# First group of a fused attention and expert kernel: keys pooled on TensorE, scores in a double bank, first two weight halves unpacked behind the first exponentials

## The chip, the cores and the metric

The kernel runs on one core of a Trainium2 chip. The metric is the device time of one execution in microseconds; lower is better. Engines are named as in the profile: PE (TensorE's matrix products) with PEld (its weight loads), DVE (VectorE), ACT (ScalarE), POOL (GpSimd), SP (the engine that issues the DMAs).

## What is computed

Three stages follow each other: attention over keys and values that are averaged in groups of eight, a dense two-layer network with a softplus, and a mixture of eight experts of which each token takes one.

```python
k_p = k.reshape(B, H, Sp, pool, D).mean(axis=3)      # pool = 8, Sp = 72, D = 64
v_p = v.reshape(B, H, Sp, pool, D).mean(axis=3)
scores = scale * np.matmul(q, k_p.transpose(0, 1, 3, 2))
attn = np.exp(scores - np.max(scores, axis=-1, keepdims=True))
attn = attn / (np.sum(attn, axis=-1, keepdims=True) + 1e-09)
x = np.matmul(attn, v_p)                             # 4608 tokens x 512
h = x @ w_in                                         # 512 x 2048
g = np.maximum(h, 0.0) + np.log1p(np.exp(-np.abs(h)))
x = g @ w_out                                        # 2048 x 512
...
y[mask] = gate_w[mask, None] * (np.maximum(xc[mask] @ w1[e], 0.0) @ w2[e])
```

## The kernel before, in words

The 4608 tokens are worked on in nine groups of 512. A group's attention consists of four **units** (`unit0` for the first group, `unit` for the others), each for two heads. A unit loads a key block of 128 x 576 and the queries, averages the keys (`keys`, L527: a DVE reduction over eight neighbours, L530), spreads the result over a block-diagonal tile (two ACT copies, L537 and L538) and forms the scores with PE (L585 in the first group, L635 later). DVE takes maxima (L593) and subtracts them (L594); `shares` (L541) has ACT's exponential (L542), DVE's sum, addition and reciprocal (L543 to L545) and POOL's multiplication (L546). In the first group PE averages the values by eight products with the identity (`pv`, L603) and transposes the shares by products with the identity (`tr`, L612); ACT copies both out of PSUM (L605, L613). `output` (L565) forms the unit's result `o` (L569), which ACT and DVE split into a rounded part `xh` and a remainder `xl` (L571, L572).

A group's dense network runs over 16 chunks of 128 hidden columns. For each, `p1` forms the hidden product in twelve matmuls (L715), ACT and DVE compute the softplus (L718 to L721) and split it (L723, L725), and `p2`, two chunks behind, adds to four output banks (L736 to L738). The bank of a hidden product comes from the pool `ps_h`, of two; it comes free when DVE's L721 has read it. In the first group that pool also holds `pv` and `o`.

The dense weights come as 64-bit words and are turned into pairs of float32 tiles while the first group is at work: `load_weights` is a generator. Its function `half` handles 512 columns of a chunk: a DMA of 512 KB (L485), two ACT unpackings (L469, L471), two DVE joins (L474, L476), an ACT copy (L491) and a DVE subtraction (L493). Chunks 4 to 15 go in pairs of 1,024 columns through the same operations (DMA L506, copy L519, subtraction L520), and two left-over halves at the end. `weights(n)` advances that generator by n steps, `STEPS` in all, and `ready(c)` tells how many steps chunk c needs.

The instructions are written in the order of these generators; a scheduler puts them into each engine's queue when the program is built, and each engine works off its queue in order. Waits are by semaphores. The order of each queue can be printed, and the section on the change does so. Lines below are those of the kernel before.

## Time and profile before

| what | value |
|---|---|
| runs shown | 1370.27, 1370.47, 1371.11 us |
| median | 1370.47 us |
| the profiled execution's own time | 1378.22 us |
| its span, first to last instruction | 1376.5 us |
| mean granted clock of TensorE | 0.994 |
| PE / PEld / DVE / ACT / POOL busy | 97% / 81% / 62% / 43% / 22% of the span |

The profile is of one execution, whose time lies 7.75 us above the median of the runs shown. Busy shares are means over the whole span, and the first hundred microseconds, in which the first group's attention and the conversion of the weights run, differ from the rest. So the trace is asked by stretch below.

### The profile page before, as it was taken

The page shows a single profiled execution, that of the slowest core. Times are in us where ns is not written, and L with a number is a line of the kernel's source. Part 1 is how long each engine was busy: PE and PEld are TensorE (multiplying, and loading weights), DVE is VectorE, ACT ScalarE, POOL GpSimd, SP SyncE. Part 2 cuts the span into 40 slices and gives each one's busy share as a digit, 9 for nine tenths or more (in the row PEclk, how much of TensorE's full clock was granted, in tenths as well). Part 3 has the DMA queues.
Part 4 walks back from the last instruction along what each step waited for, and adds up shares of the span by engine and source line. Part 5 has one row for each costly group of instructions (what it writes and reads, how often), then busy time and mean ns, then how long its engine had stood idle before and what let it go on. Part 6 is the DMA issues. An engine that isn't in the chain of part 4 may idle for free. (4 is left out here: it accounts for less than half of the span.)

```text
span 1376.5 us, 21364 instructions
## 1 busy us (share of the span) xinstructions
PE 1338.4 (97%) x7030; PEld 1114.9 (81%) x7030; DVE 847.6 (62%) x1951; ACT 594.6 (43%) x1076; POOL 309.6 (22%) x374
## 2 busy tenths in 40 slices
PE   6899999999999999999999999999999999999986
PEld 5667877777878778788778778888989898889886
DVE  7997794783974974965956847545645332325254
ACT  6985544544545545455455445541111121114142
POOL 2000012111121121030030120343424243323233
PEclk9999999999999999999999999999999999999998
DMA  8633343241241340431421301513323122225272
GB/s 283 260 115 90 86 136 75 59 130 48 76 125 35 80 129 26 112 106 31 118 70 33 106 13 47 192 39 92 96 70 100 57 76 67 81 61 169 64 269 80
DMA packets 149599, 134.16 MB, mean 97 GB/s; under 512 B 100789, under 2 KB 116789, under 8 KB 146912
## 3 DMA queue, kind: packets, MB, share of 16 engines
q1 hardware_dynamic: 131744, 95.51, 24.0%
q0 software_dynamic: 17728, 37.13, 8.5%
q8 instruction: 59, 0.97, 0.3%
q14 instruction: 68, 0.56, 0.1%
HBM read 166.67 MB, written 29.67 MB: 143 GB/s over the span
## 5 line engine op out<-in xcount | busy, mean ns | idle before, releaser
L715 PE MATMUL h<-xh,wt 128*128 128x512 f32 x1152 | 381.9, 393 | 3.4 <-DVE a L721 3.1
L715 PEld LDWEIGHTS h<-xh,wt 128*128 128x128 f32 x1152 | 217.6, 189 | 51.2 <-DVE a L721 4.9
L894 PE MATMUL h<-xt,w1h 128*128 128x256 f32 x1280 | 229.1, 282 | 4.2 <-ACT w1h L404 1.7
L736 PE MATMUL y<-wt,gh 128*128 128x512 f32 x576 | 233.2, 405 | 0.0
L119 DVE CUSTOM_DVE_ANT_0 junk<-rows,w9b 128x512 bf16<-128x512 f32 x324 | 223.0, 688 | 8.3 <-ACT rows L113 3.2
L715 PE MATMUL h<-xl,wt 128*128 128x512 f32 x576 | 225.7, 392 | 0.0
L737 PE MATMUL y<-wt,gh 128*128 128x512 f32 x576 | 225.4, 391 | 0.0
L738 PE MATMUL y<-wt,gl 128*128 128x512 f32 x576 | 224.7, 390 | 0.0
L894 PEld LDWEIGHTS h<-xt,w1h 128*128 128x128 f32 x1280 | 197.7, 189 | 9.2 <-issue 4.8
L894 PE MATMUL h<-xt,w1l 128*128 128x256 f32 x640 | 180.4, 282 | 3.8 <-issue 2.4
L898 ACT ACTIVATE hs<-h 128x512 fp32r<-128x512 f32 x80 | 47.6, 598 | 307.5 <-PE h L894 170.1
L718 ACT ACTIVATE a<-h 128x512 f32<-128x512 f32 x144 | 85.9, 597 | 184.1 <-PE h L715 172.4
L721 DVE SCALAR_TENSOR_TENSOR a<-h,a 128x512 f32<-128x512 f32 x144 | 98.5, 684 | 101.0 <-ACT a L720 100.4
L723 ACT ACTIVATE gh<-a 128x512 fp32r<-128x512 f32 x144 | 90.8, 630 | 158.5 <-DVE a L721 152.9
L736 PEld LDWEIGHTS y<-wt,gh 128*128 128x128 f32 x576 | 108.1, 188 | 36.5 <-ACT a L718 8.3
L715 PEld LDWEIGHTS h<-xl,wt 128*128 128x128 f32 x576 | 109.0, 189 | 22.9 <-issue 0.7
L738 PEld LDWEIGHTS y<-wt,gl 128*128 128x128 f32 x576 | 108.1, 188 | 23.7 <-DVE gl L725 0.4
L725 DVE TENSOR_TENSOR gl<-a,gh 128x512 fp32r<-128x512 f32 x144 | 99.2, 689 | 42.0 <-ACT gh L723 39.4
L894 PEld LDWEIGHTS h<-xt,w1l 128*128 128x128 f32 x640 | 122.7, 192 | 2.8 <-issue 1.0
L737 PEld LDWEIGHTS y<-wt,gh 128*128 128x128 f32 x576 | 108.3, 188 | 20.1 <-issue 0.4
L920 PE MATMUL y<-w2h,hs 128*128 128x512 f32 x304 | 118.4, 390 | 0.3 <-issue 0.3
L919 PE MATMUL y<-w2l,hs 128*128 128x512 f32 x304 | 118.4, 389 | 0.2 <-issue 0.2
(197 smaller groups left out, 1728.0 us busy)
## 6 DMA issues: line engine op xcount, KB each, us to landing
w9b<-w SPq DMA_DIRECT2D x81, 256.0 KB
raw<-wbits SPq DMA_DIRECT2D x12, 1024.0 KB
x2d<-rows SPq DMA_DIRECT2D x36, 260.0 KB
et<-q SPq DMA_DIRECT2D x256, 32.0 KB
kv<-kT SPq DMA_DIRECT2D x28, 288.0 KB
kv<-vT SPq DMA_DIRECT2D x28, 288.0 KB
xm<-misc SPq DMA_DIRECT2D x160, 32.0 KB
misc<-misc SPq DMA_DIRECT2D x144, 32.0 KB
```

Of the source, the lines that this page charges most:

```text
L119: nc.vector.tensor_tensor_reduce(out=ws["junk"], in0=rows[t][:, :D], in1=w9b[e], scale=1.0, scalar=0.0, op0=ALU.mult, op1=ALU.add, accum_o ...
L715: nc.tensor.matmul(h, lhsT=l, rhs=r[:, kk, :], start=n == 0, stop=n == 11)
L718: nc.scalar.activation(out=a, in_=h, func=AF.Abs)
L721: nc.vector.scalar_tensor_tensor(out=a, in0=h, scalar=0.0, in1=a, op0=ALU.max, op1=ALU.add)
L723: nc.scalar.activation(out=gh, in_=a, func=AF.Copy)
L725: nc.vector.tensor_tensor(out=gl, in0=a, in1=gh.bitcast(F32), op=ALU.subtract)
L736: nc.tensor.matmul(y, lhsT=th, rhs=wh, start=c == 0, stop=False)
L737: nc.tensor.matmul(y, lhsT=th, rhs=wl, start=False, stop=False)
L738: nc.tensor.matmul(y, lhsT=tl, rhs=wh, start=False, stop=c == 15)
L894: nc.tensor.matmul(h[:, f2, :], lhsT=l, rhs=r[:, kk, :], start=n == 0, stop=n == 11)
L919: nc.tensor.matmul(y, lhsT=hh[:, f, js], rhs=ws["w2l"][:, f, :], start=False, stop=False)
L920: nc.tensor.matmul(y, lhsT=hl[:, f, js], rhs=ws["w2h"][:, f, :], start=False, stop=f == 7)
```

## The change

In the first group, the keys are averaged by eight products with the identity on PE (`pk`, L606 of the new kernel) in place of the DVE reduction; the block-diagonal copies read that bank directly (`band`), and ACT also copies the averaged keys to SBUF for the later group that needs them (L609). All four score products of a unit go into one tile over two banks (pool `ps_s`), so that one DVE maximum (L622) and one subtraction (L623) serve the unit in place of two of each. The key products of a unit are put behind the scores of the unit before it, the value products behind the scores written last, and the unpacking of the first two weight halves behind the exponentials of the first two units (`issue_after`). The early weight halves are fetched two ahead (`fetch`), and the start advances the weights' generator in other places. The four output banks (`ps_y`) are now taken after the first group's attention has been written.

```diff
--- before.py
+++ after.py
@@ -427,7 +427,8 @@
         ep = ph.enter_context(tc.tile_pool(name="ep", bufs=1))
         ps_a = ph.enter_context(tc.tile_pool(name="ps_a", bufs=2, space=PSUM))
         ps_h = ph.enter_context(tc.tile_pool(name="ps_h", bufs=2, space=PSUM))
-        ps_y = ph.enter_context(tc.tile_pool(name="ps_y", bufs=1, space=PSUM))
+        ps_s_cm = tc.tile_pool(name="ps_s", bufs=2, space=PSUM)
+        ps_s = ps_s_cm.__enter__()
 
         kbd = []
         for i in range(2):
@@ -455,7 +456,7 @@
             return pool.tile([P, n], F32, tag=tag, name=tag)
 
         EARLY = 4
-        STEPS = 6 * EARLY + 6 * (8 - EARLY // 2)
+        STEPS = 2 + 6 * EARLY + 6 * (8 - EARLY // 2)
         scratch_cm = tc.tile_pool(name="scratch", bufs=2, side="right")
         scratch = scratch_cm.__enter__()
         wt = []
@@ -476,16 +477,22 @@
                 nc.vector.scalar_tensor_tensor(out=v, in0=hi, scalar=-0x80000000, in1=v,
                                                op0=ALU.bitwise_and, op1=ALU.bitwise_or)
 
-            def half(c, j, first):
+            def fetch(c, j):
+                raw = room("raw", 1024, True)
+                nc.sync.dma_start(out=raw.bitcast(I32), in_=bits[c * P:(c + 1) * P, j * 1024:(j + 1) * 1024])
+                return raw.bitcast(I32).rearrange("p (a b) -> p a b", b=2)
+
+            def half(c, j, raw):
                 wh, wl = (wt[c // 2][:, c % 2, i, j * 512:(j + 1) * 512] for i in range(2))
-                if first:
-                    raw = room("raw", 1024, True).bitcast(I32).rearrange("p (a b) -> p a b", b=2)
-                else:
+                if raw is None:
                     raw = scratch.tile([P, 512, 2], I32, tag="raw", name="raw")
-                nc.sync.dma_start(out=raw.rearrange("p a b -> p (a b)"),
-                                  in_=bits[c * P:(c + 1) * P, j * 1024:(j + 1) * 1024])
+                    nc.sync.dma_start(out=raw.rearrange("p a b -> p (a b)"),
+                                      in_=bits[c * P:(c + 1) * P, j * 1024:(j + 1) * 1024])
                 lo, hi = raw[:, :, 0], raw[:, :, 1]
-                unpack(lo, hi)
+                with ExitStack() as st:
+                    if c < 2 and j == 0:
+                        st.enter_context(tc.issue_after(firsts[c]))
+                    unpack(lo, hi)
                 yield
                 join(lo, lo, hi)
                 nc.scalar.activation(out=wh, in_=lo.bitcast(F32), func=AF.Copy)
@@ -496,9 +503,15 @@
 
             for i in range(EARLY // 2):
                 wt.append(wtile(i, f"wt{i}", 2, 2, 1024, dtype=F32R))
-            for c in range(EARLY):
-                for j in range(2 if c >= LAG else 1):
-                    yield from half(c, j, True)
+            early = [(c, j) for c in range(EARLY) for j in range(2 if c >= LAG else 1)]
+            raws = []
+            for i in range(2):
+                raws.append(fetch(*early[i]))
+                yield
+            for i, (c, j) in enumerate(early):
+                if i + 2 < len(early):
+                    raws.append(fetch(*early[i + 2]))
+                yield from half(c, j, raws[i])
             for i in range(EARLY // 2, 8):
                 raw = wtile(i, f"raw{i}", 2, 1024, 2, dtype=I32)
                 for j in range(2):
@@ -520,7 +533,7 @@
                     nc.vector.tensor_tensor(out=wl, in0=vs[j], in1=wh.bitcast(F32), op=ALU.subtract)
                     yield
             for c in range(LAG):
-                yield from half(c, 1, False)
+                yield from half(c, 1, None)
 
         pooled = {}
         count = [0]
@@ -531,15 +544,20 @@
                 v = kv()
                 nc.sync.dma_start(out=v, in_=vT[u])
                 pooled[u] = (kp, v, None)
-            kp = pooled[u][0]
+            return band(pooled[u][0])
+
+        def band(kp):
             kb = kbd[count[0] % 2]
             count[0] += 1
             nc.scalar.activation(out=kb[0:64, 0:SP], in_=kp[0:64, :], func=AF.Copy)
             nc.scalar.activation(out=kb[64:128, SP:2 * SP], in_=kp[64:128, :], func=AF.Copy)
             return kb
 
+        firsts, scores = [], []
+
         def shares(e, sm, rc):
-            nc.scalar.activation(out=e, in_=e, func=AF.Exp, scale=1.0 / 64)
+            ins = nc.scalar.activation(out=e, in_=e, func=AF.Exp, scale=1.0 / 64)
+            firsts.append(ins.ins)
             nc.vector.tensor_reduce(sm, e, AX.X, ALU.add)
             nc.vector.tensor_scalar_add(sm, sm, 1e-9)
             nc.vector.reciprocal(rc, sm)
@@ -579,28 +597,39 @@
             nc.sync.dma_start(out=q, in_=qT[u, :, r0:r0 + rn])
             yield
             yield
-            banks = [ps_y.tile([P, 512], F32, tag=f"y{hp % 2 * 2 + i}", name="s") for i in range(2)]
-            kb = keys(u, k, lambda: room("kv", 576, True))
+            k8 = k.rearrange("p (s w) -> p w s", w=8)
+            pk = ps_h.tile([P, 512], F32, tag="h", name="pk")[:, :SP]
+            with ExitStack() as after:
+                if scores:
+                    after.enter_context(tc.issue_after(scores[-1]))
+                for w in range(8):
+                    nc.tensor.matmul(pk, lhsT=ident, rhs=k8[:, w], start=w == 0, stop=w == 7)
+            kb = band(pk)
+            kp = pp.tile([P, SP], F32, tag="kp", name="kp")
+            nc.scalar.activation(out=kp, in_=pk, func=AF.Copy)
+            v = room("kv", 576, True)
+            nc.sync.dma_start(out=v, in_=vT[u])
+            s2 = ps_s.tile([P, 1024], F32, tag="s", name="s2")
             for t in range(T):
-                nc.tensor.matmul(banks[t // 3][:, t % 3 * 144:(t % 3 + 1) * 144],
-                                 lhsT=q[:, t * P:(t + 1) * P], rhs=kb, start=True, stop=True)
+                a = t // 2 * 512 + t % 2 * 144
+                ins = nc.tensor.matmul(s2[:, a:a + 144], lhsT=q[:, t * P:(t + 1) * P], rhs=kb, start=True, stop=True)
+            scores.append(ins.ins)
             e = k.rearrange("p (a k) -> p a k", k=SP)
             st = room("st", 24, True)
             mx, sm, rc = (st[:, i * 8:(i + 1) * 8] for i in range(3))
-            for b, (i, j) in enumerate(((0, 3), (3, 4))):
-                s3 = banks[b][:, :(j - i) * 144].rearrange("p (a k) -> p a k", k=SP)
-                m = mx[:, 2 * i:2 * j]
-                nc.vector.tensor_reduce(m, s3, AX.X, ALU.max)
-                nc.vector.tensor_tensor(out=e[:, 2 * i:2 * j], in0=s3, op=ALU.subtract,
-                                        in1=m.unsqueeze(2).to_broadcast([P, 2 * (j - i), SP]))
+            s4 = s2.rearrange("p (b x) -> p b x", b=2)[:, :, :288].rearrange("p b (a k) -> p b a k", k=SP)
+            m = mx.rearrange("p (b a) -> p b a", b=2)
+            nc.vector.tensor_reduce(m, s4, AX.X, ALU.max)
+            nc.vector.tensor_tensor(out=k.rearrange("p (b a k) -> p b a k", b=2, k=SP), in0=s4, op=ALU.subtract,
+                                    in1=m.unsqueeze(3).to_broadcast([P, 2, 4, SP]))
             shares(e, sm, rc)
             yield
             yield
-            kp, v, _ = pooled[u]
             v8 = v.rearrange("p (s w) -> p w s", w=8)
             pv = ps_h.tile([P, 512], F32, tag="h", name="pv")
-            for w in range(8):
-                nc.tensor.matmul(pv[:SP, :P], lhsT=v8[:, w], rhs=ident, start=w == 0, stop=w == 7)
+            with tc.issue_after(scores[-1]):
+                for w in range(8):
+                    nc.tensor.matmul(pv[:SP, :P], lhsT=v8[:, w], rhs=ident, start=w == 0, stop=w == 7)
             vp = pp.tile([SP, P], F32, tag="vp", name="vp")
             nc.scalar.activation(out=vp, in_=pv[:SP, :P], func=AF.Copy)
             pooled[u] = (kp, v, vp)
@@ -742,8 +771,8 @@
 
         def ready(c):
             if c < EARLY:
-                return 3 * (2 * c - min(c, LAG)) + 3
-            return 3 * (2 * EARLY - LAG) + 6 * ((c - EARLY) // 2) + 6
+                return 3 * (2 * c - min(c, LAG)) + 5
+            return 2 + 3 * (2 * EARLY - LAG) + 6 * ((c - EARLY) // 2) + 6
 
         def weights(n):
             for _ in range(n):
@@ -783,11 +812,14 @@
         feed.start(units_of(0), 1)
         for i, it in enumerate(feed.units):
             next(it)
-            if i:
+            if i % 2:
                 weights(1)
+        feed.tick()
         while feed.units or jobs:
             feed.tick()
-            weights(1)
+            weights(1 if feed.units else 2)
+        ps_s_cm.__exit__(None, None, None)
+        ps_y = ph.enter_context(tc.tile_pool(name="ps_y", bufs=1, space=PSUM))
 
         pend = []
         for g in range(NG):
```

**PE, the first group's attention up to the fourth unit's scores.** `s` are scores, `pk` and `pv` the poolings of keys and values, `tr` transposes, `o` results; a pooling and a score product each appear as twice as many instructions in the trace. Before:

```order
L585 MATMUL s<-kbd_165,boot 128x144 x4
L585 MATMUL s<-kbd_167,boot 128x144 x4
L612 MATMUL tr<-ident,boot_kv 72x128 x6
L603 MATMUL pv<-ident,boot_kv 72x128 x8
L585 MATMUL s<-kbd_165,boot 128x144 x4
L612 MATMUL tr<-ident,boot_kv 72x128 x2
L603 MATMUL pv<-ident,boot_kv 72x128 x8
L585 MATMUL s<-kbd_167,boot 128x144 x4
```

And now:

```order
L606 MATMUL pk<-boot_kv,ident 128x72 x8
L615 MATMUL s_203<-kbd_165,boot 128x144 x4
L606 MATMUL pk<-boot_kv,ident 128x72 x8
L615 MATMUL s_232<-kbd_167,boot 128x144 x4
L632 MATMUL pv<-ident,boot_kv 72x128 x8
L606 MATMUL pk<-boot_kv,ident 128x72 x8
L641 MATMUL tr<-ident,boot_kv 72x128 x8
L615 MATMUL s_272<-kbd_165,boot 128x144 x4
L632 MATMUL pv<-ident,boot_kv 72x128 x8
L606 MATMUL pk<-boot_kv,ident 128x72 x8
L641 MATMUL tr<-ident,boot_kv 72x128 x8
L615 MATMUL s_325<-kbd_167,boot 128x144 x4
```

Four key poolings stand ahead of the fourth scores that were not there, and the second unit's transposes have moved ahead of those scores; behind them the rest of the order is two value poolings, two sets of transposes and the results.

**DVE, between the third hidden chunk's L721 and the next (L750 in the new kernel).** L474 and L476 (now L475 and L477) are joins of 1,024 columns, L520 (now L533) the subtraction that ends a conversion, L653 (now L682) the transposes of a unit of the second group. Before:

```order
L721 SCALAR_TENSOR_TENSOR a<-h,a 128x512
L474 SCALAR_TENSOR_TENSOR v<-raw_516 128x1024
L653 STREAM_TRANSPOSE q<-q 128x768
L725 TENSOR_TENSOR gl<-a,gh 128x512
L476 SCALAR_TENSOR_TENSOR v<-raw_516,v 128x1024
L553 TENSOR_REDUCE vr<-kv 128x72
L520 TENSOR_TENSOR wt_567<-v,wt_567 128x1024 x2
L721 SCALAR_TENSOR_TENSOR a<-h,a 128x512
```

And now:

```order
L750 SCALAR_TENSOR_TENSOR a<-h,a 128x512
L563 RECIPROCAL st<-st 128x8
L477 SCALAR_TENSOR_TENSOR v<-raw_518,v 128x1024
L754 TENSOR_TENSOR gl<-a,gh 128x512
L682 STREAM_TRANSPOSE q<-q 128x768
L533 TENSOR_TENSOR wt_579<-v,wt_579 128x1024 x2
L475 SCALAR_TENSOR_TENSOR v<-raw_584 128x1024 x2
L477 SCALAR_TENSOR_TENSOR v<-raw_584,v 128x1024 x2
L750 SCALAR_TENSOR_TENSOR a<-h,a 128x512 x2
```

Seven operations over 1,024 columns stand between two readings of hidden banks, where four stood, and two of these readings now follow each other.

**DVE, the second unit of the second group, from its subtractions (L645, now L674) to the reduction of its values (L553, now L571).** Before:

```order
L645 TENSOR_TENSOR q<-s,st 128x2x2x72 x2
L474 SCALAR_TENSOR_TENSOR v<-raw_649 128x1024
L721 SCALAR_TENSOR_TENSOR a<-h,a 128x512
L543 TENSOR_REDUCE st<-q 128x8
L476 SCALAR_TENSOR_TENSOR v<-raw_649,v 128x1024
L544 TENSOR_SCALAR st<-st 128x8
L725 TENSOR_TENSOR gl<-a,gh 128x512
L545 RECIPROCAL st<-st 128x8
L572 SCALAR_TENSOR_TENSOR xl<-o,xh 128x512
L553 TENSOR_REDUCE vr<-kv 128x72
```

And now:

```order
L674 TENSOR_TENSOR q<-s,st 128x2x2x72 x2
L754 TENSOR_TENSOR gl<-a,gh 128x512
L475 SCALAR_TENSOR_TENSOR v<-raw_755 128x1024
L561 TENSOR_REDUCE st<-q 128x8
L477 SCALAR_TENSOR_TENSOR v<-raw_755,v 128x1024
L562 TENSOR_SCALAR st<-st 128x8
L590 SCALAR_TENSOR_TENSOR xl<-o,xh 128x512
L563 RECIPROCAL st<-st 128x8
L475 SCALAR_TENSOR_TENSOR v<-raw_755 128x1024
L682 STREAM_TRANSPOSE q<-q 128x768
L477 SCALAR_TENSOR_TENSOR v<-raw_755,v 128x1024
L571 TENSOR_REDUCE vr<-kv 128x72
```

Two more joins of 1,024 columns and the unit's transposes now stand ahead of the reduction of the values, and L721's counterpart behind it.

## Rows read from the trace of the kernel before

**Rows 1.** The page: the span, and busy time, share and instructions by engine.

```profile
span 1376.5 us, 21364 instructions
PE 1338.4 (97%) x7030; PEld 1114.9 (81%) x7030; DVE 847.6 (62%) x1951; ACT 594.6 (43%) x1076; POOL 309.6 (22%) x374
```

**Rows 2.** Stretches from:to in us; length, busy us per engine, PEclk, DMA share, GB/s.

```profile
0.00:15.24 15.24, 4.54 (x16) 3.88 (x16) 8.48 (x22) 5.99 (x11) 4.64 (x42) 1.00 0.87 304
15.24:35.60 20.36, 20.03 (x131) 16.35 (x131) 17.67 (x35) 17.64 (x37) 3.74 (x3) 1.00 0.77 274
35.60:62.50 26.90, 23.62 (x105) 18.82 (x105) 24.69 (x33) 26.85 (x39) 2.28 (x2) 1.00 0.67 266
62.50:110.00 47.50, 44.35 (x185) 32.15 (x185) 43.82 (x57) 38.21 (x61) 2.82 (x4) 0.93 0.35 112
...
200.00:800.00 600.00, 600.00 (x2809) 477.81 (x2808) 419.33 (x1087) 301.39 (x587) 97.71 (x130) 1.00 0.30 80
```

**Rows 3.** PE in order of time, 0 to 40 us: start, length, line, operation, count.

```profile
5.09 2.29 PE L585 MATMUL s<-kbd,boot 128*128 128x144 f32 x8 [5.09 <-ACT kbd L538]
...
15.24 1.50 PE L612 MATMUL tr<-ident,boot_kv 128*72 128x128 f32 x6 [5.22 <-POOL boot_kv L546]
...
19.44 1.15 PE L585 MATMUL s<-kbd,boot 128*128 128x144 f32 x8
...
20.64 2.33 PE L603 MATMUL pv<-ident,boot_kv 128*72 128x128 f32 x16
22.80 1.15 PE L585 MATMUL s<-kbd,boot 128*128 128x144 f32 x8
...
32.10 1.07 PE L612 MATMUL tr<-ident,boot_kv 128*72 128x128 f32 x8
...
35.60 0.50 PE L715 MATMUL h<-xh,wt 128*128 128x512 f32 x1 [0.32 <-DVE xl L572]
```

**Rows 4.** ACT in order of time: the first copy of a pooled key.

```profile
4.49 0.26 ACT L537 ACTIVATE kbd<-kp 64x72 f32<-64x72 f32 x1 [2.41 <-DVE kp L530]
```

**Rows 5.** PEld, 15.24 to 35.60 us, groups by form: count, busy us, mean ns.

```profile
L603 PEld LDWEIGHTS pv<-ident,boot_kv 128*72 128x72 f32 x48 | 7.6, 234 | 0.0
L612 PEld LDWEIGHTS tr<-ident,boot_kv 128*72 128x72 f32 x32 | 3.7, 125 | 7.3 <-POOL boot_kv L546 6.4 <-issue 0.8
```

**Rows 6.** DVE, 0 to 35.6 us, groups by form.

```profile
L530 DVE TENSOR_REDUCE kp<-boot_kv 128x72 f32<-128x576 f32 x4 | 3.0, 748 | 4.1 <-DMA boot_kv<-kT 4.1
L593 DVE TENSOR_REDUCE boot<-s 128x6 f32<-128x432 f32 x4 | 2.4, 605 | 1.5 <-PE s L585 1.5
L594 DVE TENSOR_TENSOR boot_kv<-s,boot 128x432 f32<-128x432 f32 x4 | 2.4, 589 | 0.0
...
L593 DVE TENSOR_REDUCE boot<-s 128x2 f32<-128x144 f32 x4 | 1.2, 299 | 0.0
L594 DVE TENSOR_TENSOR boot_kv<-s,boot 128x144 f32<-128x144 f32 x4 | 1.2, 298 | 0.0
```

**Rows 7.** DVE in order of time, 50 to 64 us.

```profile
52.96 0.69 DVE L721 SCALAR_TENSOR_TENSOR a<-h,a 128x512 f32<-128x512 f32 x1
...
59.53 2.36 DVE L520 TENSOR_TENSOR wt<-v,wt 128x1024 fp32r<-128x1024 f32 x2 [1.33 <-ACT wt L519]
61.81 0.68 DVE L721 SCALAR_TENSOR_TENSOR a<-h,a 128x512 f32<-128x512 f32 x1
```

**Rows 8.** DVE, 35.6 to 110 us, groups by form.

```profile
L474 DVE SCALAR_TENSOR_TENSOR v<-raw 128x1024 int32<-128x1024 int32 x12 | 15.3, 1285 | 0.0
L476 DVE SCALAR_TENSOR_TENSOR v<-raw,v 128x1024 int32<-128x1024 int32 x12 | 14.4, 1213 | 0.0
...
L653 DVE STREAM_TRANSPOSE q<-q 128x768 f32<-128x768 f32 x3 | 2.9, 967 | 0.0
```

**Rows 9.** PE's waits, 35.6 to 135 us: us in total, times, longest.

```profile
PE h L715 <- DVE a L721: 3.1, 3, 2.0
PE pv L560 <- DVE vr L553: 1.7, 2, 1.0
```

## The prediction

> **What bounds the kernel now.** I read the page's first lines, then the stretches of the span, then TensorE's own order of time in the first of them. PE is busy for 97% of the span [rows 1], and from 200 to 800 us without a pause [rows 2], so whatever moves the end must do so in the first hundred microseconds, where PE is not full; what is lost or won there is carried to the end. Three stretches differ. Until 15.24 PE works 4.54 us only. From 15.24 to 35.60, where the first product of the hidden layer (L715) begins, PE is busy 20.03 of 20.36 us [rows 2]: **the head of the program is bound by PE**, while DVE and ACT are at 17.7 each. From 35.60 to 110 it is the other way round: ACT is busy 26.85 of the first 26.90 us and DVE 43.82 of the next 47.50; PE idles 3.3 and 3.2 us, and its mean clock of 0.93 in the second part costs another 3.3 [rows 2].
>
> In PE's order of time [rows 3] the reader is to see two things. The same eight score instructions take 2.29 us at 5.09 and 1.15 at 19.44: the lower and the upper level of the clock (the clock column reads 1.00 for both, so I go by durations). And the distances: the fourth unit's scores begin at 22.80, its transposes at 32.10, L715 at 35.60.
>
> **The change part by part, first the head.** It takes the pooling of four keys from DVE (4 x 0.748 us) and, per unit, two maxima and two subtractions (0.605 + 0.299 + 0.589 + 0.298 = 1.79) become one of each over 576 columns, priced as the key reduction over 576 (0.75 each) [rows 6]: some 4.2 us less DVE in all. None of it is on the path after 15.24, because PE is. What it adds is on PE: per unit eight products of 72 columns, that is 16 instructions, as the value pooling's eight are. The trace has no such instruction. Upper bound: the value pooling, 2.33 us with 2.2 from its start to the next step [rows 3]. Lower bound: columns alone, half of the score's 144 columns, 1.15/8/2 = 0.07 us each, so about 1.1. I take 2.2, because both poolings read every eighth word: weight loads that step so take 234 ns against 125 for the transposes' contiguous ones [rows 5]. At the lower clock all this doubles, to about 4.3.
>
> The Trainium skill, "SBUF — State Buffer", section "Door 1: The DMA port swizzle", says that reads which cross to a new 16-byte line at each element pay a penalty, four fp32 being the free step; the keys are read eight apart. The two weight loads agree in direction, though they differ in kind as well. By that rule the price is the upper one, as taken; without it 1.1.
>
> Now PE's new order, in which nothing overtakes, with 1.0 for scores, 0.9 for transposes, 2.2 for a pooling. The first key has landed by 4.49 − 0.75 = 3.7 [rows 4, 6]. Pooling at the lower clock 4.3, to 8.0; the two copies to the block-diagonal keys 0.6 (4.49 to 5.09 [rows 3, 4]), to 8.6; scores 2.0, to 10.6; second pooling, clock rising in it, 2.8, to 13.4; copies 0.6; scores, to 15.0; value pooling, to 17.2; third pooling, to 19.4; first transposes, to 20.3, which hide the copies; scores, to 21.3; value pooling, to 23.5; fourth pooling, to 25.7; transposes, to 26.6. There the fourth unit's scores begin, 3.8 us later than at 22.80. From there before took 9.3 us to that unit's transposes (32.10), all of it PE work; now one set of transposes fewer (0.9) and half a product o more (0.4) lie between, so 8.8: 35.4. Another 3.5 to L715 as before gives 38.9; on ACT an unpacking over 1,024 columns (near 1.15) now stands right ahead of the two copies of these transposes, of which I count half, 0.6. **L715 at 39.5, +3.9.**
>
> Bounds. With 1.1 per pooling PE is no longer what waits longest: the chain of a unit through DVE, ACT and POOL is, 5.09 to 15.24 = 10.1 us from scores to transposes [rows 3]. The second scores would begin at 3.7 + 2.2 + 0.6 + 2.0 + 2.2 + 0.6 = 11.3, its transposes at 21.4, the fourth scores at 22.3: 0.5 earlier than now. If the clock stays at the lower level to about 18, as before (at 15.24 six transposes take 1.50 us, at 32.10 eight take 1.07 [rows 3]), scores, value pooling and the rest until there double: about 3.4 more, +7.3.
>
> The rest of the head costs nothing: four more copies of pooled keys on ACT (near 0.26 each, as the copy at 4.49) behind the block-diagonal ones, with ACT idle there for 2.4 us before such a copy [rows 4]; should that go, they delay the next activation by one copy. The wait of the first two unpackings for the exponentials holds up on ACT two pairs of 0.67 us, whose weights meet their first use at L715, far behind. On SP the second weight half passes two value loads and two 1 MB loads pass the fourth half, so that is later by some microseconds; its first user is the second layer, behind 2 chunks. POOL has the same four multiplications.
>
> **The stretch from 35.60 to 110.** DVE's order changes in two places. Between two L721 (now L750) before stood 8.85 us (52.96 to 61.81), with 1.33 of it waiting for ACT, and PE, which needs L721 for a free bank, lost 2.0 [rows 7, 9]. Now there stand 0.68 + 0.20 + 1.21 + 0.68 + 0.97 + 2.36 + 2 x 1.285 + 2 x 1.213 = 11.1 us (the long ones by [rows 7, 8], the L754 priced as the L750, 0.2 a small reciprocal's allowance), less some 0.1 of overlap for each of 11: 10.0. So the loss is 1.2 larger. In the unit after that, between the subtractions and the reduction of values that PE waits for, two conversions (1.285 + 1.213) and the stream transpose (0.97) [rows 8] are added and one L721 (0.68) is gone: 2.8 more, less a wait of some 0.8 that PE now has near there (three waits for L721 are 3.1, the longest 2.0 [rows 9]): +2.0. The clock loses 3.3 us here now; I leave that as it is, give or take 1.7 for one low stretch more or fewer. Against it stands that ACT has more of the next conversion done when L715 begins: four long unpackings instead of one, 3 x 1.15 = 3.5, which shortens PE's 3.3 us of idling at best [rows 2]; since DVE's order sets the two waits, I count 0.4. Sum of the stretch: 1.2 + 2.0 − 0.4 = **+2.8**.
>
> **Sum.** 3.9 + 2.8 = +6.7 us. The profiled execution takes 1378.22, so 1384.9; it is 7.75 above the median of the runs shown, 1370.47, which becomes **1377.2**. A measurement of this kernel can tell about 0.2%, 2.7 us.
>
> **Rivals.** (a) *Faster.* The pooling takes little more than its columns and the clock rises early, so L715 comes 0.5 earlier, and the conversions that are ahead remove PE's idling of 3.3 before 62.5: −3.8, 1366.7. Its place is PE's head, and it decides at about 1.3 us per pooling. For it: DVE loses 4.2 us of work. Against it: PE is full from 15.24, and the stepping loads are slow [rows 5]. I give 0.14. The Trainium skill, "TensorE: Matmul & The Clock Gate", section "What's actually happening", has activity release the low clock; earlier and denser PE work would then end the low level sooner. No row of before can show it; by it scores one (2.0 to 1.0) and pooling two (2.8 to 2.2) give back 1.6, which belongs to this rival and to the low side of my forecast.
> (b) *No change.* The head is late by 3.9, but ACT and DVE bound what follows, and ACT's 3.5 us of work done ahead give most of it back: +0.4, 1370.9. For it: ACT is full from 35.6 to 62.5. Against it: the long run of DVE work ahead of the two L750. 0.13.
> (c) *Slower still.* The clock stays low to about 18 (+3.4) or falls once or twice more after the new gaps: 1377.2 + 3.4 to 1377.2 + 6.8, about 1382. For it: the clock did not rise with 4.5 us of work before 15.24. 0.13.
> (d) That the parts don't do what they say I can exclude from the order: the exponential does stand ahead of the unpacking on ACT, and the key products are on PE.
>
> **How the numbers follow.** The forecast (1377.2, own range 1373.5 to 1381) has 0.60; (a) 0.14, (b) 0.13, (c) 0.13. The range drops (a) and reaches through (b) to most of (c): 1369.5 to 1383.5, with about 0.18 outside. Faster by over 0.2% (below 1367.7) is (a), 0.14; within 0.2% is (b), 0.13; slower is the forecast and (c), 0.73.
>
> **What would show it.** In the changed profile: PE busy nearly without a pause from about 4 us to the first L744, and that at 38 to 41 us; 16 instructions of a key pooling in about 2.2 us at the upper clock; the fourth scores near 26.6; a PE wait for L750 of 3 us or more near 66, and one for L571 of 2 or more near 92. The prediction is wrong if a pooling takes 1.3 us or less, if L744 begins before 36, or if PE's idling from there to 110 us falls under 5.

## The result, and the profile after

The changed kernel takes 1379.5 us (median of 4, 1378.3 to 1380.63), the kernel before 1370.37 beside it (1369.67 to 1371.11): ratio 1.0066, interval 1.0049 to 1.0084. It is slower by 9.1 us; the forecast was 1377.2 against 1370.47, so 6.7.

The first lines of the changed kernel's page, to be held against [rows 1]:

```profile
span 1377.6 us, 21492 instructions
PE 1347.6 (98%) x7094; PEld 1125.2 (82%) x7094; DVE 843.7 (61%) x1939; ACT 595.0 (43%) x1080; POOL 312.5 (23%) x374
```

PE has 64 instructions and 9.2 us of busy time more, DVE 3.9 us less. The spans are nearly equal because the profiled execution of before was 7.75 us above its median, in its last third (from the 141st of the 144 hidden products to the end it takes 487.5 us, the changed kernel 480.2; a hidden product is the twelve matmuls of one chunk, L715 before and L744 now). So I compare the times at which products start, not the spans. The stretches of the changed kernel, with the columns of [rows 2]:

```profile
0.00:15.24 15.24, 10.18 (x44) 9.81 (x45) 2.04 (x7) 3.35 (x9) 3.05 (x41) 1.00 0.86 295
15.24:35.60 20.36, 20.05 (x138) 18.85 (x138) 17.53 (x28) 16.30 (x34) 3.45 (x3) 1.00 0.68 237
35.60:62.50 26.90, 26.29 (x119) 18.52 (x119) 23.96 (x38) 26.48 (x44) 3.56 (x3) 1.00 0.84 341
62.50:110.00 47.50, 39.41 (x160) 29.66 (x159) 44.46 (x52) 39.28 (x62) 1.88 (x2) 0.89 0.30 88
```

PE's order of time in the head (compare [rows 3]; L606 is the key pooling, L615 the scores, L632 the value pooling, L641 the transposes, L744 the hidden product):

```profile
3.93 3.66 PE L606 MATMUL pk<-boot_kv,ident 128*128 128x72 f32 x16 [3.93 <-DMA boot_kv<-kT]
8.15 2.29 PE L615 MATMUL s<-kbd,boot 128*128 128x144 f32 x8 [0.56 <-ACT kbd L553]
10.24 3.53 PE L606 MATMUL pk<-boot_kv,ident 128*128 128x72 f32 x16
14.33 2.29 PE L615 MATMUL s<-kbd,boot 128*128 128x144 f32 x8 [0.56 <-ACT kbd L553]
16.41 3.49 PE L632 MATMUL pv<-ident,boot_kv 128*72 128x128 f32 x16
19.74 2.29 PE L606 MATMUL pk<-boot_kv,ident 128*128 128x72 f32 x16
...
29.45 1.16 PE L615 MATMUL s<-kbd,boot 128*128 128x144 f32 x8
...
38.94 1.07 PE L641 MATMUL tr<-ident,boot_kv 128*72 128x128 f32 x8
...
42.71 0.50 PE L744 MATMUL h<-xh,wt 128*128 128x512 f32 x1
```

PE works from 3.93 nearly without a pause, and what it works on takes the length of the lower clock level until 19.74. L744 starts at 42.71 in place of 35.60. Behind it, PE's waits from 42.8 to 140 us (against [rows 9]):

```profile
PE pv L578 <- DVE vr L571: 4.3, 1, 4.3
PE s L664 <- ACT kbd L553: 3.8, 1, 3.8
PE h L744 <- DVE a L750: 0.3, 1, 0.3
```

Two long waits stand in place of several short ones. PE where they end:

```profile
70.74 0.69 PE L664 MATMUL s<-kbd,q 128*64 128x144 f32 x2 [3.81 <-ACT kbd L553]
...
96.23 0.40 PE L578 MATMUL pv<-ident,vr 128*72 128x128 f32 x1 [4.29 <-DVE vr L571]
```

The first lies at 66.9 to 70.74. DVE (first four rows) and ACT (last four) in order of time there:

```profile
59.61 0.68 DVE L750 SCALAR_TENSOR_TENSOR a<-h,a 128x512 f32<-128x512 f32 x1
...
66.10 2.35 DVE L475 SCALAR_TENSOR_TENSOR v<-raw 128x1024 int32<-128x1024 int32 x2
68.37 2.35 DVE L477 SCALAR_TENSOR_TENSOR v<-raw,v 128x1024 int32<-128x1024 int32 x2
70.64 1.43 DVE L750 SCALAR_TENSOR_TENSOR a<-h,a 128x512 f32<-128x512 f32 x2
...
67.07 1.17 ACT L470 ACTIVATE raw<-raw 128x1024 f32<-128x1024 f32 x1
68.10 1.16 ACT L472 ACTIVATE raw<-raw 128x1024 int32<-128x1024 uint32 x1
69.12 0.61 ACT L747 ACTIVATE a<-h 128x512 f32<-128x512 f32 x1
...
70.43 0.26 ACT L553 ACTIVATE kbd<-kp 64x72 f32<-64x72 f32 x1
```

From one L750 to the next pass 11.03 us, most of them conversions (8.85 from one L721 to the next before [rows 7]), and on ACT the unpackings stand ahead of the copy that PE's next scores need. That copy ends at 70.69; the L744 behind the scores, at 71.38, needs the first of the two L750, which ends near 71.3. So mending either alone would save little there; this is read from the times and was not run. The clock fell at the end of the first wait and within the second: 0.50 was granted from 70.8 to 74.2 and from 94.7 to 101.5.

**An account for all runs.** From each trace I took the start of the first hidden product, the sum of PE's pauses from there to the thirtieth, and how long the lower clock was granted in that time. Half of that last time is counted as lost: in the changed kernel matmuls of 512 columns begin 0.23 us apart at the upper level (64.28 to 64.51) and 0.43 at the lower (71.97 to 72.40). What then remains from first to thirtieth lies between 173.9 and 175.7 us in every kernel, so these three numbers carry a difference to within 1.8 us. From the thirtieth to the 141st pass 667.3 us in every kernel but e4 and e11 (668.5), so what is late at the thirtieth stays late (8.4 us here). Each row is one execution, and the lower clock differs between executions: the mean granted clock of e9's eleven runs lies between 0.993 and 0.998, and its row is the run with 0.998. In the table, "fill" are unused products that keep PE busy; the hold is explained with e3.

| kernel | ratio to before, interval | first | pauses | low clock | thirtieth |
|---|---|---|---|---|---|
| before | 1 | 35.6 | 7.2 | 6.8 | 221.7 |
| the change | 1.0066 (1.0049 to 1.0084) | 42.7 | 8.4 | 10.2 | 230.1 |
| e1 change, keys on DVE | 1.0051 (1.0037 to 1.0064) | 34.6 | 13.2 | 10.2 | 228.1 |
| e2 before, key products | 1.0045 (1.0031 to 1.0058) | 45.1 | 6.0 | 3.4 | 227.2 |
| e3 change, old generator | 1.0057 (1.0043 to 1.0070) | 46.8 | 6.0 | 0 | 228.2 |
| e4 before, fill | 0.9992 (0.9982 to 1.0001) | 35.8 | 5.9 | 3.4 | 219.0 |
| e5 neither | 1.0002 (0.9992 to 1.0011) | 37.2 | 5.7 | 6.8 | 220.5 |
| e6 e1 without the hold | 1.0040 (1.0026 to 1.0053) | 36.5 | 10.6 | 10.2 | 226.2 |
| e7 change, fill | 1.0100 (1.0085 to 1.0116) | 44.5 | 8.9 | 6.8 | 232.5 |
| e8 before, values on POOL | 1.0043 (1.0029 to 1.0058) | 37.6 | 8.5 | 13.7 | 227.0 |
| e9 fetching ahead alone | 0.9963 (0.9949 to 0.9977) | 36.4 | 4.6 | 0 | 215.7 |
| e10 change, keys in rows | 1.0067 (1.0041 to 1.0092) | 41.3 | 10.7 | 10.2 | 231.4 |
| e11 e5 with fill | 1.0014 (0.9998 to 1.0029) | 36.2 | 6.8 | 3.4 | 219.8 |
| e12 e9 with key products | 1.0041 (1.0023 to 1.0060) | 47.4 | 3.2 | 3.4 | 226.3 |

The sets ran apart: the kernel before took 1370.09 us beside e1 to e4, 1383.09 beside e5 to e8, 1379.75 beside e9 to e11, 1382.28 beside e12. Only ratios are compared across sets; times in us in the expectations of e5 to e8 were written for a kernel before of 1370.4.

### The profile page after: what moved, and what is told of

It reads as the page before. It is cut to its first block, busy times and chain, and to the rows that moved or that the text cites. A ratio compares the mean times of both kernels' runs of the same rounds, so it can differ in the third digit from the quotient of the medians.

```text
span 1377.6 us, 21492 instructions
## 1 busy us (share of the span) xinstructions
PE 1347.6 (98%) x7094; PEld 1125.2 (82%) x7094; DVE 843.7 (61%) x1939; ACT 595.0 (43%) x1080; POOL 312.5 (23%) x374
## 5 line engine op out<-in xcount | busy, mean ns | idle before, releaser
L744 PE MATMUL h<-xh,wt 128*128 128x512 f32 x1152 | 382.7, 393 | 0.4 <-DVE a L750 0.3
L744 PEld LDWEIGHTS h<-xh,wt 128*128 128x128 f32 x1152 | 217.8, 189 | 48.5 <-DVE a L750 1.1
L744 PE MATMUL h<-xl,wt 128*128 128x512 f32 x576 | 225.7, 392 | 0.0
L750 DVE SCALAR_TENSOR_TENSOR a<-h,a 128x512 f32<-128x512 f32 x144 | 98.6, 685 | 110.2 <-ACT a L749 109.5
L744 PEld LDWEIGHTS h<-xl,wt 128*128 128x128 f32 x576 | 109.1, 189 | 23.5 <-issue 1.4
L954 DVE SCALAR_TENSOR_TENSOR ys<-y,xg 128x512 f32<-128x512 f32 x38 | 28.5, 751 | 147.2 <-PE y L952 147.2
```

The costliest lines, as they stand in the source:

```text
L744: nc.tensor.matmul(h, lhsT=l, rhs=r[:, kk, :], start=n == 0, stop=n == 11)
L750: nc.vector.scalar_tensor_tensor(out=a, in0=h, scalar=0.0, in1=a, op0=ALU.max, op1=ALU.add)
```

## The experiments

### Each half of the change alone (e1 to e4)

e1: the changed kernel with the keys averaged by DVE.

```diff
...
-                for w in range(8):
-                    nc.tensor.matmul(pk, lhsT=ident, rhs=k8[:, w], start=w == 0, stop=w == 7)
-            kb = band(pk)
...
-            nc.scalar.activation(out=kp, in_=pk, func=AF.Copy)
+            nc.vector.tensor_reduce(kp, k.rearrange("p (s w) -> p s w", w=8), AX.X, ALU.add)
+            kb = band(kp)
```

> The changed kernel with one part undone: in the first group DVE averages the keys again (one reduction of about 0.75 us per unit), no key product is left on PE. Theory P (the head is bound by PE and the key products, 2.3 us each at the upper clock level and 3.5 at the lower, make it late): the first hidden product comes back from 42.7 to about 35 us; the two long waits of PE behind it (3.8 and 4.3 us in the changed kernel) come from the changed place of the weights' conversion and stay, so about 3 to 5 us over the kernel before: near 1374. Rival R (the double bank and the ordered starts make the head late, the key products are cheap): the first hidden product stays near 42 us and the time near 1379. Rival S (everything follows from the late head, the two waits too): 35 us and the time of the kernel before, 1370.

e2 is the reverse: the kernel before with only the key products and the copies that go with them.

> The kernel before with one part alone: the keys of the first group are averaged by eight products with the identity on PE, their copies read PSUM, ACT makes the SBUF copy; scores in two banks apiece, the weights' conversion and all orders as before. Theory P: the head is late by 6 to 10 us (first hidden product at 42 to 46 us), and the time is 1376 to 1382. Rival R (key products cheap, other parts guilty): first hidden product at 36, time within 2 us of 1370.4.

e3: the changed kernel with the weights' generator as before (no fetching ahead, no hold, steps in the old places). The hold is what keeps the first two unpackings behind the exponentials.

```diff
...
-                with ExitStack() as st:
-                    if c < 2 and j == 0:
-                        st.enter_context(tc.issue_after(firsts[c]))
-                    unpack(lo, hi)
+                unpack(lo, hi)
...
-            for i, (c, j) in enumerate(early):
-                if i + 2 < len(early):
-                    raws.append(fetch(*early[i + 2]))
-                yield from half(c, j, raws[i])
+            for c, j in early:
+                yield from half(c, j, fetch(c, j))
...
-            if i % 2:
+            if i:
                 weights(1)
-        feed.tick()
         while feed.units or jobs:
             feed.tick()
-            weights(1 if feed.units else 2)
+            weights(1)
```

> The changed kernel with the weights' generator as it was: each half is fetched in its own step, no unpacking waits for an exponential, the steps between the units as before; key products and the double bank stay. Theory P: the head stays late (first hidden product at 42 to 44 us), while the two long waits behind it shrink from 8.1 us to about 3, so that the stretch up to 110 us gives part of the delay back: 1372 to 1375. Rival S (the waits follow from the late head): both stay, 1378 to 1380.

e4: the kernel before with eleven unused products of the identity with itself, to see what the clock alone is worth.

```diff
...
+            if hp == 1:
+                fl = ps_a.tile([P, 512], F32, tag="pa", name="fill")
+                with tc.issue_after(ins.ins):
+                    for _ in range(11):
+                        nc.tensor.matmul(fl[:, :P], lhsT=ident, rhs=ident, start=True, stop=True)
```

> The kernel before with eleven products of the identity with itself on PE right behind the second unit's scores, where PE idles from 10 to 15.2 us; their result is read by nothing. Theory P (the head is one chain of PE work from 15.2 us on, part of it at the lower clock level): the clock rises before the first transposes, these and the first value pooling take 3.4 us rather than 4.6, the first hidden product comes at 33 to 34.5 us rather than 35.6, the time falls by 1 to 4 us, to 1366.5 to 1369.5. Rival C (the early clock level does not matter, because DVE and ACT set the pace): no change, 1370.4.

The head behaved as theory P said: without the key products the hidden layer starts at 34.6, with them at 45.1 or 46.8, whatever the generator. The time of e2 came as P expected, but those of e1 and e3 did not (1377.41 for near 1374, 1378.24 for 1372 to 1375). e1 gave back 8.1 us of head and only 2.0 at the thirtieth product, since 4.8 us of pauses came instead and the remainder is 1.2 longer; e3 lost its low clock and 2.4 us of pauses and gained 1.9, since its head is 4.1 later and the remainder 1.6 longer. **The costs of the two halves do not add**: each alone leaves 0.45 to 0.57%, both make 0.66%. PE in e4:

```profile
15.56 1.07 PE L617 MATMUL tr<-ident,boot_kv 128*72 128x128 f32 x8 [0.87 <-POOL boot_kv L546]
...
34.15 0.46 PE L640 MATMUL s<-kbd,q 128*64 128x144 f32 x2 [0.86 <-ACT boot L618]
```

The clock rose early, and the fourth scores began at 21.76, 1.0 us before their time; but at 34.15 PE waited 0.86 us for an ACT copy, and neither the first hidden product (35.8) nor, with certainty, the time moved. So PE alone does not bound the end of the head: a gain of 1 us on PE was lost there.

### Neither half, and the hold (e5, e6)

e5 is e1 and e3 together; of the change it has the score tile over two banks and the place of the value products. e6 is e1 without the hold (the first edit of e3's diff).

> The changed kernel without its two suspects: keys averaged on DVE again and the weights' generator of before (no fetching ahead, unpackings not held, steps as before). What is left of the change is the score tile over two banks, the one maximum and subtraction per unit, and the place of the value products. Theory T (the key products and the generator's new order are the only two causes): the first hidden product at 34 to 37 us, the thirtieth at 219 to 223, time 1368 to 1372.5. Rival D (the score tile over two banks, with its maximum waiting for all four products, has a price of its own): the thirtieth at 225 or later, time 1374 or more.

> The changed kernel with keys averaged on DVE, and the first two unpackings no longer held behind the exponentials; fetching ahead and the new steps stay. Theory O (the hold alone puts the long run of DVE work together): no PE wait above 2 us between 40 and 100 us, time 1370 to 1373. Rival F (fetching ahead and the steps do it): PE waits between 40 and 100 us that add up to over 7 us, the thirtieth hidden product at 226 or later, time 1375.5 to 1378.5.

e5 is at 1.0002 (0.9992 to 1.0011), as theory T said: the score tile has no price that can be measured, and the two halves are all there is. e6 keeps PE waits of 2.0, 3.5 and 3.8 us, as rival F said, so fetching ahead or the moved steps make them. In these two traces the hold adds 1.9 us at the thirtieth product, but the intervals of e1 and e6 overlap.

### Fetching ahead against the moved steps (e9)

Three lines differ from e6; fetching ahead is the only part of the generator's change that is left.

```diff
-            if i % 2:
+            if i:
                 weights(1)
-        feed.tick()
         while feed.units or jobs:
             feed.tick()
-            weights(1 if feed.units else 2)
+            weights(1)
```

> The changed kernel with keys averaged on DVE, the first unpackings not held, and the start of the program advancing the generator as before: of the generator's changes only the fetching two ahead is left. Theory Q (the steps written at other places set DVE's long runs; fetching ahead costs nothing): PE waits between 40 and 100 us under 5 us in all, the thirtieth hidden product within 1.5 us of where the neither-run had it (219 to 222), ratio to before 0.9985 to 1.0015. Rival R (fetching ahead does it, since the conversion of pairs gets ahead of the softplus): waits of 7 us or more, the thirtieth at 225 or later, ratio 1.003 to 1.006.

Theory Q holds in that fetching ahead makes no long waits, but its numbers were missed: the thirtieth product comes at 215.7 and not at 219 to 222, and e9 is **faster than both kernels**, by 0.37% of before. Its stretches, 35.6 to 62.5 and 62.5 to 110 us:

```profile
35.60:62.50 26.90, 25.34 (x116) 20.69 (x114) 25.60 (x34) 26.90 (x38) 1.41 (x2) 1.00 0.61 243
62.50:110.00 47.50, 45.02 (x204) 33.26 (x203) 44.97 (x57) 39.65 (x65) 3.91 (x4) 1.00 0.36 114
```

DVE does as much as in the changed kernel (44.97 against 44.46 us), but PE works 45.02 us in place of 39.41 and keeps its upper clock. The place of the long run on DVE, first in e6, then in e9:

```profile
56.55 0.68 DVE L740 SCALAR_TENSOR_TENSOR a<-h,a 128x512 f32<-128x512 f32 x1
...
62.63 2.35 DVE L475 SCALAR_TENSOR_TENSOR v<-raw 128x1024 int32<-128x1024 int32 x2
64.90 2.35 DVE L477 SCALAR_TENSOR_TENSOR v<-raw,v 128x1024 int32<-128x1024 int32 x2
67.17 1.28 DVE L740 SCALAR_TENSOR_TENSOR a<-h,a 128x512 f32<-128x512 f32 x2
```

```profile
58.32 0.65 DVE L740 SCALAR_TENSOR_TENSOR a<-h,a 128x512 f32<-128x512 f32 x1
...
66.96 0.68 DVE L740 SCALAR_TENSOR_TENSOR a<-h,a 128x512 f32<-128x512 f32 x1
...
73.91 0.69 DVE L740 SCALAR_TENSOR_TENSOR a<-h,a 128x512 f32<-128x512 f32 x1
```

With the steps moved, 10.62 us pass between two softplus operations; with them in place 8.64 and 6.95. PE's longest wait in e9, from 36.5 to 140 us:

```profile
PE h L734 <- DVE a L740: 2.1, 2, 1.6
```

The three lines are worth 10.5 us at the thirtieth product (226.2 to 215.7): 6.0 of pauses and half of 10.2 of low clock, less 0.7 of remainder. Which of the three lines does it was not tried. Fetching ahead alone (e5 to e9) gains 4.8, most of it the 6.8 us of low clock that do not occur in this execution; its fourth long unpacking starts at 43.59, that of e5 at 48.88.

### The key products in the good order (e12)

> The fetch-only run with the keys averaged on PE again, that is, the changed kernel without the held unpackings and with the generator advanced at the old places. Theory K (the key products keep their own price, whatever order follows): the first hidden product at 42 to 46 us, the thirtieth 4 us or more behind the fetch-only run's 215.7, that is at 220 or later, ratio to before 1.000 to 1.005, so above the fetch-only run's whole interval. Theory S (only the moved steps and the held unpackings did harm, and slack behind the head absorbs the key products): first hidden product 42 to 46 as well, but the thirtieth at 214 to 218 and PE waits between 40 and 100 us under 4 us, ratio 0.995 to 0.998.

Theory K came true: the pauses are the fewest of all, and still the thirtieth product is 10.6 us behind e9, the first 11.0. PE in order of time, and ACT at that place:

```profile
3.96 3.66 PE L603 MATMUL pk<-boot_kv,ident 128*128 128x72 f32 x16 [3.96 <-DMA boot_kv<-kT]
13.05 2.29 PE L612 MATMUL s<-kbd,boot 128*128 128x144 f32 x8 [5.43 <-ACT kbd L550]
```

```profile
9.30 0.65 ACT L470 ACTIVATE boot<-boot 128x512 f32<-128x512 f32 x1 [7.21 <-DMA boot<-wbits]
...
11.98 0.66 ACT L495 ACTIVATE wt<-boot 128x512 fp32r<-128x512 f32 x1 [1.49 <-DVE boot L477]
12.54 0.21 ACT L549 ACTIVATE kbd<-pk 64x72 f32<-64x72 f32 x1
```

The pooled keys are done at 7.6, but ACT's queue has the first unpacking and its copy ahead of the block-diagonal copies, and the first unpacking waits for its DMA until 9.30. In the changed kernel the hold takes these away (copies at 7.63) and L744 starts 4.7 us sooner. So hold and moved steps serve the key products: 4.7 us in front, while the moved steps cost 10.5 behind in e6 against e9. With the key products the two together lose 3.8 us at the thirtieth product (230.1 against 226.3). The hold without the moved steps was not tried.

### The price of a key product, and the clock (e7, e10, e8, e11)

e10 reads 72 neighbouring words per product instead of every eighth.

```diff
-            k8 = k.rearrange("p (s w) -> p w s", w=8)
+            k8 = k.rearrange("p (w s) -> p w s", w=8)
```

> The changed kernel with the eight key products of a unit reading 72 neighbouring words each instead of every eighth word; other keys are then averaged together, so the scores are others, and nothing else is changed. Theory E (reading every eighth word makes a key product dear): 16 instructions take at most 1.5 us at the upper clock level and at most 3 at the lower, the first hidden product at 38 to 40.5, ratio to before 1.003 to 1.0055. Rival I (the price is that of sixteen short instructions, however they read): 2.1 to 2.4 us and 3.4 to 3.8 as in the changed kernel, first hidden product 42 to 44, ratio 1.0055 to 1.0085.

PE, e10, a pooling at either clock level:

```profile
3.78 3.66 PE L606 MATMUL pk<-boot_kv,ident 128*128 128x72 f32 x16 [3.78 <-POOL tok_i L87]
...
18.77 1.90 PE L606 MATMUL pk<-boot_kv,ident 128*128 128x72 f32 x16
```

At the lower level the step costs nothing (3.66 both ways), at the upper 0.39 of 2.29 us. Rival I came true at the lower level and in the ratio, at the upper level neither theory did. There the step makes up a sixth of the price; most of it is that of sixteen short instructions with their weight loads. What is loaded for a key product is the identity, which lies contiguous either way: such a load takes 208 ns in the changed kernel and 193 in e10 at the upper level, 332 in both at the lower. The time does not show the difference.

e7 gives PE unused products from 1.53 us on.

```diff
+                else:
+                    fl = ps_a.tile([P, 512], F32, tag="pa", name="fill")
+                    wide = ident.unsqueeze(1).to_broadcast([P, 4, P])
+                    nc.tensor.matmul(fl.rearrange("p (a b) -> p a b", a=4), lhsT=ident, rhs=wide, start=True, stop=True)
+                    for _ in range(2):
+                        last = nc.tensor.matmul(fl[:, :P], lhsT=ident, rhs=ident, start=True, stop=True)
+                    after.enter_context(tc.issue_after(last.ins))
```

> The changed kernel with three products of the identity with itself (one of 512 columns, two of 128) ahead of the first key product, while PE would have nothing to do; their result is not used. Theory W (the low clock is a good half of the head's delay, and denser work before 4 us ends it sooner): the clock rises before 14 us, the first hidden product at 38 to 40.5, time 1375.5 to 1378. Rival N (what is done before 4 us doesn't matter, the low level lasts as long as the key and value products do): clock rises at 18 to 21, first hidden product 42 to 44, time 1378.5 to 1381.

```profile
4.25 3.53 PE L613 MATMUL pk<-boot_kv,ident 128*128 128x72 f32 x16
8.34 2.29 PE L622 MATMUL s<-kbd,boot 128*128 128x144 f32 x8 [0.56 <-ACT kbd L553]
10.42 3.53 PE L613 MATMUL pk<-boot_kv,ident 128*128 128x72 f32 x16
16.99 2.29 PE L622 MATMUL s<-kbd,boot 128*128 128x144 f32 x8 [3.04 <-ACT kbd L553]
...
21.81 2.29 PE L613 MATMUL pk<-boot_kv,ident 128*128 128x72 f32 x16
```

Rival N came true for the clock: PE had something to do from 1.53 to 13.9 with one pause of 0.56, and its products kept the longer durations into the second scores at 16.99. For the time (1.0100) the run says nothing, since an unpacking came ahead of the second copies and PE waited 3.04 for them.

e8 takes the value pooling off PE, in the kernel before.

```diff
-            for w in range(8):
-                nc.tensor.matmul(pv[:SP, :P], lhsT=v8[:, w], rhs=ident, start=w == 0, stop=w == 7)
+            v3 = v.rearrange("p (s w) -> p s w", w=8)
+            for n in (4, 2, 1):
+                nc.gpsimd.tensor_tensor(out=v3[:, :, :n], in0=v3[:, :, :n], in1=v3[:, :, n:2 * n], op=ALU.add)
+            nc.tensor.matmul(pv[:SP, :P], lhsT=v8[:, 0], rhs=ident, start=True, stop=True)
```

> The kernel before, with the eight value products of each unit of the first group replaced by three additions on POOL and one product with the identity; the change's opposite, since it takes some 2 us of work per unit off PE. Theory H (PE bounds the head, and the head is carried to the end): the first hidden product at 28 to 32 us, the thirtieth at 216 to 219, time 1364 to 1368.5. Rival C (behind the head the conversion of the weights on ACT and DVE takes the gain back): first hidden product 28 to 32 as well, but new PE waits before 70 us, the thirtieth at 220 to 223, time 1369 to 1372. Rival G (the additions on POOL hold up the multiplication of the shares): first hidden product 36 or later, time 1372 or more.

```profile
22.54 1.07 PE L614 MATMUL tr<-ident,boot_kv 128*72 128x128 f32 x8 [1.09 <-POOL boot_kv L546]
...
28.51 1.92 PE L614 MATMUL tr<-ident,boot_kv 128*72 128x128 f32 x8 [1.69 <-POOL boot_kv L546]
30.36 2.78 PE L569 MATMUL o<-boot,vp 72*64 72x512 f32 x4
```

POOL at the third multiplication:

```profile
26.96 1.49 POOL L546 TENSOR_TENSOR boot_kv<-boot_kv,boot 128x576 f32<-128x576 f32 x1 [2.82 <-DVE boot L545]
```

Rival G came true: the additions of three units ran in one piece on POOL (nine, 6.32 us) ahead of the second multiplication, and PE waited 1.09 for it. The third multiplication had no addition to wait for, but DVE's reciprocal; the exponential ahead of that started at 24.34 on ACT, behind the copies of the late transposes, and PE waited 1.69. In this second wait the clock fell (granted 0.50 from 27.4 to 41.0): the same transposes took 1.07 and then 1.92. A unit's value products went from 2.33 to 0.43 us or a little more, and yet the hidden layer began 2.0 us later than before.

e11 is e5 with e4's fill.

> The neither-run (score tile over two banks and place of the value products, old keys, old generator) with eleven unused products of the identity with itself behind the second unit's scores, as tried on the kernel before. Theory C (the fill ends the low clock sooner, which the one-maximum order can use): the clock rises before 15 us, the first hidden product at 32.5 to 35.5, the thirtieth 216 to 219.5, ratio to before 0.9955 to 0.999. Rival Z (what bounds the stretch behind the head takes it back): first hidden product 35.5 to 37.5, ratio 0.999 to 1.0015.

```profile
8.98 2.62 PE L605 MATMUL fill<-ident 128*128 128x128 f32 x22
15.31 0.64 PE L630 MATMUL tr<-ident,boot_kv 128*72 128x128 f32 x2 [3.71 <-POOL boot_kv L555]
15.74 3.38 PE L621 MATMUL pv<-ident,boot_kv 128*72 128x128 f32 x16
```

Rival Z's numbers came (1.0014, 0.9998 to 1.0029; first hidden product at 36.2), but the run does not test theory C. The fill ran at the upper level (2.62 us, 4.58 in e4), PE then waited 3.71 us for POOL, and the granted clock was 0.50 from 15.3 to 18.7, so that the first value pooling took 3.38 us. An upper clock in that stretch, which theory C supposes, occurred in e4 alone.

## Why the prediction was right

The direction, the sum's size (6.7 forecast, 8.4 at the thirtieth product, 9.1 in the medians) and both places hold, and none of the three signs that would have refuted it came. Two of the signs for it were missed: the fourth scores came at 29.45 and not near 26.6, and L744 at 42.71 and not at 38 to 41. That the sum came so near is in part luck: its first term was too small (3.9, measured 7.1) and its second too large (2.8, measured 1.3).

- **Price of a key pooling**: 2.2 from its start to the next step at the upper clock against 2.11 (19.74 to 21.85; 2.29 long); at the lower level 4.3 against 3.53 to 3.66, so it does not double. The reason given for 2.2, "because both poolings read every eighth word", was mostly wrong, and the number right by luck: the step is 0.39 of it (e10), and the weight load, from which the price was argued, does not step in a key product. The Trainium skill, "SBUF — State Buffer", section "Door 1: The DMA port swizzle", has a penalty for each access that crosses to a new 16-byte line. Of that e10 shows these 0.39 us at the upper level and nothing at the lower.
- **The head**: L744 at 39.5 against 42.71. The step that failed is "second pooling, clock rising in it, 2.8". It ran 3.53, and the scores and the value pooling behind it at lower lengths too: from 10.24 to 19.74 passed 9.5 us, where the forecast has 6.6 (10.6 to 17.2). That is 2.9 of the 3.2 missing; the case stood there as a bound (+3.4, so +7.3 for L744, which came 7.1 later). For the clock, the Trainium skill, "TensorE: Matmul & The Clock Gate", section "What's actually happening", has activity release the lower level. The traces bear that out only in part. The changed kernel, busy from 3.93 us on but for two pauses of 0.56, kept the lower level to 16.4 and beyond; e7, busy from 1.53 to 13.9 but for one, kept it beyond 16.99. In e4, with its fill from 10.10, the transposes took 1.07 at 15.56, without gain for the first hidden product. Why the lower level lasted so long stays open.
- **Behind the head**: +2.8 forecast; first to thirtieth product took 187.4 against 186.1, +1.3. The two waits came, at 70.74 (3.81, forecast 3.2 near 66) and 96.23 (4.29, forecast 2 or more near 92), but most of the short waits of before went, and the pauses grew by 1.2 only. The clock, left "as it is", lost another 1.7; the remaining 1.6 the other way I cannot assign.
- **"since DVE's order sets the two waits"**: that the places of the generator's steps set them is shown by e6 against e9: with the generator advanced at the old places the waits are 1.6 at most. That ACT releases the first of them, within a microsecond of DVE, was not foreseen, and whether DVE's order would set it without ACT's is not shown.
- **That the terms add** was wrong. Alone, each half costs more at the thirtieth product than its term: the key products 5.5 us (e2), the generator's new order 6.4 (e1); together they make 8.4. The key products cost 2.0 us on top of the new generator (e1 to the change) and 10.6 on top of fetching ahead alone (e9 to e12). As I read it, a late head leaves the conversions more time, and a kernel that is going to wait for them anyway loses less by it; the pauses agree (13.2 us in e1, 8.4 in the change), but no run tests it by itself.
- **Rival (b)**'s mechanism, conversions that are ahead, is real (e5 to e9), but it was in fetching the weights earlier and was covered by the moved steps.

## What to carry to other kernels

Where two engines bound successive stretches, ablate the parts of a change both from the old and from the new kernel: here the same part cost 2 or 10.6 us, and one part of a losing change (fetching two ahead, e9 at 0.9963 against e5 at 1.0002) was a gain that the others hid. Steps of a generator that are written in other places can join long conversions into one run; look for the longest distance between two operations that free what PE needs. Work taken off an engine helps only if nothing else makes it pause: in e8 PE waited instead, and its clock fell in one of the waits.

## What the runs showed that was not expected

- The lower clock did not double the short key products: eight of them with their loads took 3.53 to 3.66 against 2.29 us, while the scores took 2.29 against 1.16 to 1.25.
- PE busy 10.18 of the first 15.24 us did not end the lower level in the changed kernel; it ended between 16.4 and 19.74. In the kernel before, with 4.54 us, it ended at about the same time, by 19.44 [rows 2, 3].
- In e8, three additions over 288, 144 and 72 elements took POOL 1.70 us for the last unit and 6.32 for three units in a row, more than its multiplication of 576 elements (1.15 to 1.69).
